# A mixer block with a long convolution: a compact constant expanded on ScalarE, q loaded by two rows, and a permutation moved up in the second chunk

## The chip, the cores and the metric

The kernel runs on one core of a Trainium2 chip. The metric is the device time of one execution in microseconds. A core has TensorE (PE, matmuls into PSUM), VectorE (DVE), ScalarE (ACT) and GpSimd (POOL) for elementwise work, and SyncE (SP), whose queue issues most of the DMA transfers here. Each engine takes its instructions in the order of the program. They wait for each other only where data or a buffer calls for it.

## The reference

All data is fp32, with S = 2048 tokens and D = 640 channels. The first half is a long causal convolution with a gate, the second a token-mixing MLP:

```python
mod = (silu(c) @ w_mod).reshape(1, 6, 1, -1)
sa, ca, ga, sb, cb, gb = (mod[:, i] for i in range(6))
h = layernorm(x) * (1 + ca) + sa                        # x = q
kv = causal_conv4(k, shift_k) * v                       # per channel
y = irfft(rfft(kv, 4096) * rfft(ssm_k, 4096))[:2048] + kv * ssm_D
x = x + ga * (h * y)
h = layernorm(x) * (1 + cb) + sb
x = x + gb * (gelu(layernorm(h).T @ w1 + b1) @ w2 + b2).T
```

## The kernel before

The channels are worked in five chunks of 128. Within a chunk each half of 64 channels is handled on its own. The convolution is a discrete transform in two steps, both as small fp32 matmuls, for the signal and for the filter.

- `step1(side, t)` is the first step: 32 matmuls into one PSUM buffer, then one ScalarE evacuation into `Z`. Side 0 is the signal (from `X`, or from `X1` for chunk 1), side 1 the filter, from `KSP`, which lies in tile `P`. Four calls make a side.
- `f2(g)`, eight calls per chunk, is the second step for both sides: 64 matmuls against the constant `W2` (tiles `w0` for g below 4 and `w1` for the others). ScalarE copies the filter's half to `kt`, VectorE makes two products into `P` (two buffers in turn), and POOL, or VectorE for the last g, adds them into `Y`.
- `i2(r)` and `i1(half)` are the two steps back. `i2` fills two PSUM buffers, which ScalarE evacuates in four instructions. `gate(c, ps, half)` multiplies the result of `i1` by the normalised q (`A1`) and adds it to x.

`psum()` hands out three PSUM buffers in turn. A matmul group that takes a buffer waits until the group three calls before it has been read.

Beside the transforms of one chunk, the next chunk's products kv are computed (`kv_ops`, on VectorE and, for one quarter, on POOL), and later chunks' rows of k and v are loaded (`kv_loads`, `load_k`, `load_v`). `load_ks(c)` loads chunk c's filter, `perm_add` (POOL) adds `ssm_D` to it, and `perm` (ScalarE, 128x2048) lays it out in `KSP`.

The order is written out by hand. Start: rows of k and v and the filter for chunk 0 (lines 450 to 461), kv for chunk 0, then the two halves of `W2` between the loads for chunk 1 (lines 481 and 483), `perm(0)`, and step one. In the loop over chunks (line 549) the calls of `f2` are mixed with other work. At the end of chunk 0, `load_q` (line 495) loads all of q into tiles `xa` and `xb`, 16 rows per partition; one DMA is one row for 64 partitions. Then `q_stats` makes the row statistics.

The modulation vectors of the first half are computed in chunk 1. `mod_load` fetches five pieces of `w_mod`, each of which needs a place: the first three go to `X1`, `KSR` and the start of `T_in`, the others wait until a place has been read. `mod_part` multiplies one piece into the PSUM tile `tap` (12 matmuls), `mod_sum` copies the sum out, and `mod_row(i)` spreads a row over 128 partitions with matmuls on one partition. `late(n)` then applies gate and normalisation to chunk 0, which could not be done before, and `ac`/`po` prepare `A1` of chunk 1 on ScalarE and VectorE.

The tile `xa` is empty until `load_q`.

Of the kernel before, what the change touches and what calls it, by code (L numbers as in the profile page):

```python
# [20 lines left out]
def _constants():  # L21
# [20 lines left out]
    sel = np.zeros((128, 128))  # L42
    sel[0, 0:64] = sel[1, 64:128] = 1
    small = np.concatenate([f1.reshape(128, 256), v2, np.eye(128)[:, 0:36], sel], 1)
    return {"small": small.astype(np.float32), "w2": w2.reshape(128, 8192).astype(np.float32),
# [4 lines left out]
def mixer_kernel(ctx: ExitStack, tc: tile.TileContext, q, k, v, shift_k, ssm_k, ssm_D, w1, b1, w2, b2, c,  # L50
# [49 lines left out]
    SM = T_v1[:, 4096:4516]  # L100
    F1, V2, ID = SM[:, 0:256], SM[:, 256:384], SM[:, 384:420]
# [354 lines left out]
    sync.dma_start(SM, dram(c_small, 0, [[548, 128], [1, 420]]))  # L456
# [22 lines left out]
    kv_loads(1, 2)  # L479
    run(kv_ops(3))  # L480
    sync.dma_start(T_w2[0], c_w2[:, 0:4096], max_dma_last_dim=4096)
# [13 lines left out]
    def load_q():  # L495

        for j in range(16):
            for b in range(2):
                sync.dma_start(XH[j // 8][64 * b:64 * b + 64, j % 8], dram(q, (16 * b + j) * D, [[32 * D, 64], [1, D]]))  # L499
# [33 lines left out]
    pl = [t[:, 0:1920] for t in (X1, KSR, T_in, KSR, T_in)]  # L533
# [15 lines left out]
    for c in range(NC):  # L549
# [3 lines left out]
        for g in range(8):  # L553
# [665 lines left out]
```

## Time and profile before

| | us |
|---|---|
| three runs | 702.47, 696.88, 701.62 |
| median of the runs | 701.62 |
| the profiled execution | 699.95 |
| its span | 698.1 |

The profiled execution is a fourth one. The profile's times count from the start of its span; the 1.85 us between span and execution lie around it. Where the stages of the first chunks lie, by TensorE's timeline:

| stage | begins, us |
|---|---|
| first matmul of step one, chunk 0 | 23.30 |
| `f2`, chunk 0 | 40.16 |
| first step back, chunk 0 | 62.77 |
| `f2`, chunk 1 | 91.68 |
| first step back, chunk 1 | 119.39 |
| filter's step one for chunk 2 | 146.91 |
| `f2`, chunk 2 | 158.42 |

Busy times over the span:

```profile
PE 624.4 (89%) x9099; PEld 597.3 (86%) x9099; DVE 494.4 (71%) x881; ACT 293.8 (42%) x469; POOL 139.5 (20%) x161
```

PEld is the loading of weights, which overlaps the matmuls. A busy share is an average over stages with different limits. What an edit is worth has to be read in its own stage: which wait ends last there, and what stands next behind it. In a timeline row the columns are the start, the duration, the engine, the line of the kernel, the operation, what it writes and reads, and a count where neighbours are merged. The brackets hold the idle time before and what ended it.

### The profile page before, as it was taken

The numbers are of one execution on the slowest core, as the hardware profiler recorded it, in microseconds if no ns is written. First come the engines' busy times: TensorE is split into PE (matmuls) and PEld (weight loads), VectorE is DVE, ScalarE is ACT, GpSimd is POOL, SyncE is SP. The second block draws the span as 40 slices with busy tenths as digits, with TensorE's granted clock in tenths as the row PEclk, the third lists the DMA queues.
The fourth block names the chain that finished last, engine by engine and source line by source line (L and its number), as shares of the span: only waits on it lengthen the run. The fifth ranks groups of instructions, "written<-read, shape, count | busy, mean of one in ns | idle before, by whom it ended". The sixth has DMA issues, their size and how long they took to land.

```text
span 698.1 us, 20773 instructions
## 1 busy us (share of the span) xinstructions
PE 624.4 (89%) x9099; PEld 597.3 (86%) x9099; DVE 494.4 (71%) x881; ACT 293.8 (42%) x469; POOL 139.5 (20%) x161
## 2 busy tenths in 40 slices
PE   0689889978799988888799999999999989999997
PEld 0688886868798878678799979999999989999997
DVE  7857976578959539888985841123399968888985
ACT  0544562665536636456666232233244233333331
POOL 5176423259125025000100000000000430000000
PEclk9999999889999999999999999999999999999999
DMA  9998788575433524161305504433353533466611
GB/s 179 242 222 222 193 254 236 119 161 124 85 73 102 164 64 122 59 152 31 60 1 92 117 5 93 89 61 62 106 143 105 158 129 100 121 171 172 174 36 38
DMA packets 166931, 84.38 MB, mean 121 GB/s; under 512 B 91030, under 2 KB 157368, under 8 KB 166840
## 3 DMA queue, kind: packets, MB, share of 16 engines
q1 hardware_dynamic: 162220, 81.72, 46.8%
q10 hardware_dynamic: 4620, 1.33, 1.1%
q8 instruction: 71, 1.16, 0.7%
q14 instruction: 20, 0.16, 0.1%
HBM read 72.55 MB, written 10.49 MB: 119 GB/s over the span
## 4 chain that ended last, share of the span: by engine, by line
PE 60%; DVE 18%; DMA 6%; ACT 5%; SPq 4%; issue 3%; POOL 3%; ACTq 0%; POOLq 0%; DVEq 0%
PE pst L438 20%; PE pst L1078 17%; PE pst L1155 7%; PE pst L220 5%; PE pst L264 4%; SPq L499 3%; DVE tap L59 3%; DVE p L59 3%; PE pst L235 3%; DVE kt L59 2%; DMA in<-in_A_k_dram 2%; DMA in<-in_A_v_dram 2%; PE pst L284 2%; PE tap L344 1%; DVE aux L59 1%
## 5 line engine op out<-in xcount | busy, mean ns | idle before, releaser
L235 PEld LDWEIGHTS pst<-z,w 128*64 128x64 f32 x2560 | 76.8, 138 | 18.3 <-issue 9.8
L235 PE MATMUL pst<-z,w 128*64 128x64 f32 x2560 | 79.2, 223 | 14.7 <-issue 5.6
L59 DVE TENSOR_TENSOR p<-pst,kt 128x512 f32<-128x512 f32 x80 | 51.2, 681 | 18.1 <-ACT kt L239 14.1
L222 ACT ACTIVATE z<-pst 128x1024 f32<-128x1024 f32 x40 | 42.9, 1073 | 46.5 <-PE pst L220 46.5
L59 POOL TENSOR_TENSOR y<-p 128x256 f32<-128x256 f32 x72 | 51.1, 739 | 49.1 <-DVE p L59 48.9
L220 PE MATMUL pst<-v,x 128*64 128x128 f32 x512 | 35.3, 301 | 27.6 <-DVE x L59 27.6
L220 PEld LDWEIGHTS pst<-v,x 128*64 128x64 f32 x512 | 32.5, 154 | 29.9 <-POOL t L465 23.3
L220 PE MATMUL pst<-v,p 128*64 128x128 f32 x640 | 40.3, 290 | 5.3 <-ACT p L163 4.4
L239 ACT ACTIVATE kt<-pst 128x512 f32<-128x512 f32 x40 | 23.9, 598 | 48.5 <-PE pst L235 33.1
L1078 PE MATMUL pst<-r_z,m_w 128*128 128x320 f32 x222 | 42.0, 312 | 2.2 <-DVE m_w L59 2.2
L220 PEld LDWEIGHTS pst<-v,p 128*64 128x64 f32 x640 | 38.5, 147 | 6.2 <-ACT p L163 4.6
L914 ACT ACTIVATE pst<-pst,sm 128x640 f32<-128x640 f32 x13 | 10.0, 767 | 75.9 <-PE pst L438 75.9
L264 PEld LDWEIGHTS pst<-v,y 32*128 32x128 f32 x1280 | 38.5, 189 | 3.9 <-issue 2.9
L264 PE MATMUL pst<-v,y 32*128 32x64 f32 x1280 | 40.4, 274 | 0.4 <-issue 0.3
L1066 ACT ACTIVATE m_w<-m_v 128x896 fp32r<-128x896 f32 x24 | 22.7, 951 | 36.9 <-PE pst L1078 16.8
L59 POOL TENSOR_TENSOR m_p<-u_i,r_z 128x320 f32<-128x320 f32 x1 | 0.9, 876 | 183.4 <-issue 183.4
L1078 PEld LDWEIGHTS pst<-r_z,m_w 128*128 128x128 f32 x222 | 35.2, 190 | 2.4 <-DVE m_w L59 2.4
L59 DVE TENSOR_TENSOR tap<-tap,kt 128x512 f32<-128x512 f32 x48 | 33.4, 697 | 1.2
L59 DVE TENSOR_TENSOR kt<-in,tap 128x512 f32<-128x512 f32 x48 | 32.9, 686 | 1.5
L273 ACT ACTIVATE z<-pst 128x512 f32<-128x512 f32 x38 | 20.9, 648 | 22.5 <-PE pst L264 22.5
L284 PEld LDWEIGHTS pst<-z,v 64*64 64x64 f32 x1280 | 22.2, 144 | 9.4 <-issue 5.8
L284 PE MATMUL pst<-z,v 64*64 64x64 f32 x1280 | 24.1, 229 | 6.7 <-issue 4.1
(301 smaller groups left out, 1483.7 us busy)
## 6 DMA issues: line engine op xcount, KB each, us to landing
x<-in_B_w_dram SPq DMA_DIRECT2D x20, 512.0 KB
aux<-in_A_ssm_k_dram SPq DMA_DIRECT2D x10, 512.0 KB
in<-in_A_k_dram SPq DMA_DIRECT2D x36, 128.0 KB
in<-in_A_v_dram SPq DMA_DIRECT2D x36, 128.0 KB
m_x<-xs SPq DMA_DIRECT2D x28, 160.0 KB
out_dram<-m_x SPq DMA_DIRECT2D x28, 160.0 KB
w<-in_const_w_dram SPq DMA_DIRECT2D x2, 2048.0 KB
m_v<-in_B_w_dram SPq DMA_DIRECT2D x9, 448.0 KB
```

The costliest lines, as they stand in the source:

```text
L59: TT = lambda eng, o, a, b, op: eng.tensor_tensor(o, a, b, op=op)
L220: pe.matmul(ps[64 * ri:64 * ri + 64, o:o + 255:2], lhs, F1[:, 128 * ri:128 * ri + 128], start=True, stop=True)
L222: evac = lambda: act.activation(Z[:, side, t], ps.rearrange("p (a k e) -> p a k e", a=4, e=2), AF.Copy)
L235: pe.matmul(ps[64 * h:64 * h + 64, o:o + 64], W2[k1 // 32][:, 2 * (k1 % 32) + ri], rhs, start=True, stop=True)
L239: act.activation(kt.rearrange("p (m i) -> p m i", i=32), pv[:, :, 1], AF.Copy)
L264: pe.matmul(pp[qd // 2][:, o:o + 64], Y[p, ri, i:i + 2].rearrange("p i k -> p (i k)"), V2[p, 64 * ri:64 * ri + 64], start=ri == 0, stop=ri ...
L284: pe.matmul(ps[64 * b:64 * b + 64, 512 * e + 64 * jj:512 * e + 64 * jj + 64], V1[p, ri, n2], T2[p, :, 32 * ri + n2], start=ri == 0, stop=r ...
L438: pe.matmul(ps[0:m, h, 0:320], w_.bitcast(F32R), r_[:, 320 * h:320 * h + 320].bitcast(F32R), start=first and i == 0, stop=last and i == 2)
L499: sync.dma_start(XH[j // 8][64 * b:64 * b + 64, j % 8], dram(q, (16 * b + j) * D, [[32 * D, 64], [1, D]]))
L1066: act.activation(W[n][0].bitcast(F32R), A[p, w_], AF.Copy)
L1078: pe.matmul(bank[n], w[:, i].bitcast(F32R), r.bitcast(F32R), start=i == 0 and k == 0, stop=i == 6 and k == 2)
L1155: pe.matmul(acc[s][:, h, 0:320], w[:, f_].bitcast(F32R), u[r + h].bitcast(F32R), start=f_ == 0 and k == 0, stop=f_ == NF - 1 and k == 2)
```

## The change

Three parts.

1. `W2` held, for each column of the transform, a copy of the coefficients for one channel of a pair and zeros for the other. The constant is now stored without the zeros, 128x4096 in place of 128x8192. Its two halves are loaded into the tile `xa`, and ScalarE lays them out in `W2`. Each instruction (`w2_part`) writes the columns of one channel, scaled per partition by 1 or 0 (`OWN`, two new columns of the small constant). Half 0 takes two instructions around step one, half 1 takes four in the first three calls of `f2`. The two loads also stand earlier in SP's queue.
2. `load_q` loads two rows per DMA. A copy of eight rows from `q` to `xs` in device memory precedes it; `xs` is overwritten later by the spilled x.
3. In chunk 1, `mod_part` starts one call of `f2` earlier, so that four of the five lie in the loop. The places of the fourth and fifth piece change, and the filter of chunk 2 is loaded in the loop. `mod_sum` writes to `T_z` in place of `P`, which lets `perm(2)` run before the first step back. The three `mod_row` calls move ahead of that step, too.

```diff
-    w2 = np.zeros((2, 32, 2, 64, 2, 2, 32))
-    for c in range(2):
-        w2[0, :, c, :, 0, c] = np.cos(ang)
-        w2[1, :, c, :, 0, c] = -np.sin(ang)
-        w2[0, :, c, :, 1, c] = np.sin(ang)
-        w2[1, :, c, :, 1, c] = np.cos(ang)
+    w2 = np.zeros((2, 32, 2, 64, 2, 32))
+    w2[0, :, :, :, 0] = np.cos(ang)[:, None]
+    w2[1, :, :, :, 0] = -np.sin(ang)[:, None]
+    w2[0, :, :, :, 1] = np.sin(ang)[:, None]
+    w2[1, :, :, :, 1] = np.cos(ang)[:, None]
...
+    own = np.arange(128)[:, None] % 2 == np.arange(2)
+    small = np.concatenate([f1.reshape(128, 256), v2, np.eye(128)[:, 0:36], own], 1)
...
+    def w2_load(i):
+        sync.dma_start(T_x[0][:, 2048 * i:2048 * i + 2048], c_w2[:, 2048 * i:2048 * i + 2048])
+
+    def w2_part(i, c_, o=0, n=64):
+        act.activation(T_w2[i].rearrange("p (m c k) -> p c m k", c=2, k=32)[:, c_, o:o + n],
+                       T_x[0][:, 2048 * i + 32 * o:2048 * i + 32 * (o + n)].rearrange("p (m k) -> p m k", k=32),
+                       AF.Identity, scale=OWN[:, c_:c_ + 1])
...
     run(kv_ops(2, pool))
+    w2_load(0)
     run(kv_ops(0))
     kv_loads(1, 0)
     run(kv_ops(1))
     kv_loads(1, 1)
     kv_loads(1, 2)
+    w2_load(1)
     run(kv_ops(3))
-    sync.dma_start(T_w2[0], c_w2[:, 0:4096], max_dma_last_dim=4096)
     kv_loads(1, 3)
-    sync.dma_start(T_w2[1], c_w2[:, 4096:8192], max_dma_last_dim=4096)
     perm_add(0)
     perm(0)
+    w2_part(0, 0)
     all_taps()
     for t in range(4):
         step1(0, t)
+        if t == 1:
+            w2_part(0, 1)
...
-        for j in range(16):
+        sync.dma_start(dram(xs, 0, [[8 * D, 8], [1, 8 * D]]), dram(q, 0, [[8 * D, 8], [1, 8 * D]]))
+        for j in range(0, 16, 2):
             for b in range(2):
-                sync.dma_start(XH[j // 8][64 * b:64 * b + 64, j % 8], dram(q, (16 * b + j) * D, [[32 * D, 64], [1, D]]))
+                sync.dma_start(XH[j // 8][64 * b:64 * b + 64, j % 8:j % 8 + 2],
+                               dram(q, (16 * b + j) * D, [[32 * D, 64], [D, 2], [1, D]]))
...
-    pl = [t[:, 0:1920] for t in (X1, KSR, T_in, KSR, T_in)]
+    pl = [t[:, 0:1920] for t in (X1, KSR, T_in, X1, T_in)]
...
+            if c == 0 and g < 3:
+                for i in ((0, 1), (2,), (3,))[g]:
+                    w2_part(1, i % 2, 32 * (i // 2), 32)
...
-                if g > 4:
-                    mod_part(tap, g - 5, three(pl[g - 5]))
-                    if g > 5:
-                        mod_load(0, g - 3, pl[g - 3])
+                if g > 3:
+                    mod_part(tap, g - 4, three(pl[g - 4]))
+                if g == 4:
+                    mod_load(0, 3, pl[3])
+                if g == 6:
+                    mod_load(0, 4, pl[4])
+                    load_ks(2)
...
             step1(0, 0)
-            mod_part(tap, 3, three(pl[3]))
-            load_ks(2)
+            mod_part(tap, 4, three(pl[4]))
+            mod_sum(tap, T_z[:, 5120:5760])
             step1(0, 1)
-            mod_part(tap, 4, three(pl[4]))
...
             q_newton(3)
-            mod_sum(tap, P[:, 0:640])
+            mod_row(0, T_z[:, 5120:5760])
+            mod_row(1, T_z[:, 5120:5760])
+            perm_add(2)
+            perm(2)
+            load_ks(3)
+            mod_row(2, T_z[:, 5120:5760])
             i2(0)
-            mod_row(0, P[:, 0:640])
-            mod_row(1, P[:, 0:640])
-            mod_row(2, P[:, 0:640])
             run(late(2)[0] + ac[0:4])
...
             spill(0)
-            perm_add(2)
-            perm(2)
-            load_ks(3)
             taps()
```

More of the change, by code (lines that the diff above doesn't have):

```diff
@@ L41, in _constants @@
     v1 = np.tile(np.stack([np.cos(ang), np.sin(ang)], 1).reshape(64, 4096) / 2048, (2, 1))
[L42 to L45, printed above, removed]
+    own = np.arange(128)[:, None] % 2 == np.arange(2)
+    small = np.concatenate([f1.reshape(128, 256), v2, np.eye(128)[:, 0:36], own], 1)
+    return {"small": small.astype(np.float32), "w2": w2.reshape(128, 4096).astype(np.float32),
             "v1": v1.astype(np.float32)}
@@ L99, in mixer_kernel @@
     V1 = T_v1[:, 0:4096].rearrange("p (r n m) -> p r n m", r=2, n=32)
-    SM = T_v1[:, 4096:4516]
-    F1, V2, ID = SM[:, 0:256], SM[:, 256:384], SM[:, 384:420]
+    SM = T_v1[:, 4096:4518]
+    F1, V2, ID, OWN = SM[:, 0:256], SM[:, 256:384], SM[:, 384:420], SM[:, 420:422]
     TR, DR = T_rows[:, 0:256], T_rows[:, 512:576]
@@ L455, in mixer_kernel @@
         load_v(0, g, both)
-    sync.dma_start(SM, dram(c_small, 0, [[548, 128], [1, 420]]))
+    sync.dma_start(SM, dram(c_small, 0, [[422, 128], [1, 422]]))
     load_ks(0, act)
```

## The prediction

> **What bounds the kernel now.** I read the page's chain of waits first, then the timelines of the engines and of SP's queue over the first 200 us, because every edit lies in the program's first 160 us. What comes after is the same code, and it starts when these stages end.
>
> ```profile
> PE 60%; DVE 18%; DMA 6%; ACT 5%; SPq 4%; issue 3%; POOL 3%; ACTq 0%; POOLq 0%; DVEq 0%
> ```
>
> TensorE holds most of the path. So an edit counts where TensorE stands still in the stages it touches, or where it takes work off TensorE. There are three such places. The first is the second transform (`f2`) of chunk 0. POOL computes a quarter of chunk 1's product there, and only then makes the additions that free `f2`'s buffers:
>
> ```profile
> 38.29 2.50 POOL L59 TENSOR_TENSOR t<-in,t 128x512 f32<-128x512 f32 x2 [15.15 <-DMA in<-in_A_v_dram]
> ...
> 48.86 6.98 POOL L59 TENSOR_TENSOR y<-p 128x256 f32<-128x256 f32 x10
> ```
>
> ```profile
> 49.63 1.39 DVE L59 TENSOR_TENSOR p<-pst,kt 128x512 f32<-128x512 f32 x2 [2.95 <-POOL y L59]
> ```
>
> POOL stood 15.15 us for a transfer, so its additions begin at 48.86, and VectorE's third product of `f2` waits 2.95 us for them. The second place is the end of chunk 1, in TensorE's own timeline:
>
> ```profile
> 102.48 2.08 PE L235 MATMUL pst<-z,w 128*64 128x64 f32 x64 [1.25 <-DVE p L59]
> ...
> 118.18 1.28 PE L344 MATMUL tap<-in,sm 128*32 128x320 f32 x12 [0.24 <-DMA in<-in_w_mod_dram]
> 119.39 3.80 PE L264 MATMUL pst<-v,y 32*128 32x64 f32 x128
> 123.01 4.83 PE L355 MATMUL pst<-p,sm 1*128 1x320 f32 x12
> 127.77 3.68 PE L220 MATMUL pst<-v,x 128*64 128x128 f32 x32
> 131.38 4.21 PE L264 MATMUL pst<-v,y 32*128 32x64 f32 x128
> 135.52 1.97 PE L220 MATMUL pst<-v,x 128*64 128x128 f32 x32
> ...
> 146.91 3.68 PE L220 MATMUL pst<-v,p 128*64 128x128 f32 x32 [4.44 <-ACT p L163]
> 150.93 6.34 PE L220 MATMUL pst<-v,p 128*64 128x128 f32 x96 [0.34 <-DVE aux L59]
> ```
>
> The columns are start, duration, instructions, and in brackets the idle time before and what ended it. The wait of 4.44 us for the permutation (ACT `p`) looks like the prize. But the 96 matmuls after it start only at 150.93, when the gate (DVE `aux`) has freed a PSUM buffer. The permutation lies beside the gate's own chain. The third place is two gaps with no releaser:
>
> ```profile
> 48.86 1.33 PE L235 MATMUL pst<-z,w 128*64 128x64 f32 x38 [2.06 <-issue]
> ...
> 81.00 1.31 PE L284 MATMUL pst<-z,v 64*64 64x64 f32 x41 [2.19 <-issue]
> ```
>
> Both fall while long-row transfers run (the second half of `w`, and `q`). I take them, as a guess, for TensorE waiting for its own instructions.
>
> **Step two's matrix.** Removed are two loads of 2.1 MB. Added are two of 1.05 MB and six ScalarE instructions. In SP's queue:
>
> ```profile
> 18.93 1.85 SPq L137 DMA_DIRECT2D in<-in_A_v_dram  x2
> ...
> 27.31 0.64 SPq L481 DMA_DIRECT2D w<-in_const_w_dram  x1
> 28.05 1.54 SPq L131 DMA_DIRECT2D in<-in_A_k_dram  x2
> ```
>
> The k and v rows that POOL waits for are issued from 28.05, right behind the first `w` load. After the change the same 2.1 MB is ahead of them, but half of it is issued at 18.93 or earlier, and the engines have room there:
>
> ```profile
> 20.00:28.00 8.00, 4.70 (x58) 4.73 (x60) 5.82 (x10) 4.44 (x3) 1.43 (x2) 1.00 0.76 166
> 30.00:34.00 4.00, 4.00 (x78) 4.00 (x76) 3.79 (x7) 2.37 (x3) 0.00 (x0) 1.00 1.02 410
> ```
>
> The last two numbers of a row are the DMA share and GB/s. From 20 to 28 us the 16 engines are 0.76 busy, so (1 - 0.76) x 8 = 1.9 us is free. Behind that, `w` moves at 410 GB/s, so one load takes 1.05 MB / 410 GB/s = 2.6 us. POOL's rows come earlier by what the free time absorbs: 1.9 us, at most 2.6, and nothing if its wait is paced by something else on SP's queue. I take 1.9 because that room is a measured share. It is less than the 2.95 us that VectorE waits, so all of it passes on to the end of `f2`, and TensorE, busy from there to 90 us, carries it on. What is late next is ScalarE's copy of `f2`'s result, which the new instructions share.
>
> ```profile
> 22.84 2.06 ACT L163 ACTIVATE p<-aux 128x2048 f32<-128x2048 f32 x1
> ...
> 28.58 1.09 ACT L222 ACTIVATE z<-pst 128x1024 f32<-128x1024 f32 x1 [0.66 <-PE pst L220]
> ...
> 44.16 0.60 ACT L239 ACTIVATE kt<-pst 128x512 f32<-128x512 f32 x1 [1.27 <-PE pst L235]
> ```
>
> Two of the instructions take 2048 elements, like the permutation at 22.84 (2.06 us each), and four take 1024, half of that (1.03 each): 8.2 us in all. The first is queued behind the permutation, so ready at 24.9, and all eight evacuations of step one stand behind it. Its load is issued by 18.93 + 0.64 = 19.6 and needs 2.6 us of engines that are no longer full then, so it lands between 22 and 24. Step one gives ScalarE one evacuation per 1.09 + 0.66 = 1.75 us, and three PSUM buffers are in turn. Part, two evacuations, part, third evacuation take 2 x 2.06 + 3 x 1.09 = 7.4 us. TensorE wants the third buffer again at 28.58 + 3 x 1.75 = 33.8, so the cover is gone only if the load lands after 26.4, and then the cost is one for one. The other four follow the evacuations of `f2`, between which ScalarE idles 1.27 us. They make the second evacuation under 1 us late, inside VectorE's 2.95 us wait. I cost ScalarE's work at nothing.
>
> **q by two rows.** 32 issues become 17, behind one copy from `q` into `xs` on eight engines.
>
> ```profile
> 73.22 12.45 SPq L499 DMA_DIRECT2D xa<-in_A_q_dram  x16
> 85.71 11.54 SPq L499 DMA_DIRECT2D xb<-in_A_q_dram  x16
> ```
>
> SP issues q for 24.0 us, 5.24 MB, so 218 GB/s. Behind it stand the loads of `w_mod`. The change starts q sooner and at best halves it. On TensorE's path the late loads cost only the 0.24 us at 118.18, so the edit is worth 0.24 us, and nothing if q is no faster. The spill of chunk 0, which overwrites what the copy put into `xs`, is issued after all of q has been used.
>
> **Chunk 1's order.** Before, three `mod_part`s lie in `f2` and two behind it. After, four and one. The extra one (1.28 us) fits the gap of 1.25 us at 102.48, so the loop is no longer. Step one's second group then ends at 117.94 as before, with the last `mod_part` already done. From there, before: 0.24 + 1.28, inverse 3.80, rows 4.83, step one 3.68, inverse 4.21, end 135.6. After: rows, inverse, evacuation of both its PSUM buffers with step one beside it, inverse. The clock decides what these cost:
>
> ```profile
> 118.00:124.00 6.00, 5.82 (x144) 4.64 (x144) 0.00 (x0) 2.50 (x4) 0.50 (x2) 1.00 1.06 171
> 124.00:127.00 3.00, 2.91 (x9) 1.78 (x8) 0.00 (x0) 3.00 (x7) 0.00 (x0) 0.74 0.65 148
> 127.00:130.00 3.00, 3.00 (x24) 2.23 (x24) 2.02 (x3) 2.67 (x7) 0.00 (x0) 0.50 0.82 185
> 130.00:133.00 3.00, 3.00 (x58) 2.67 (x54) 2.90 (x5) 1.08 (x1) 1.10 (x1) 0.62 0.20 46
> ```
>
> The third number from the end is the granted clock. At 0.50 for the rest of 124 to 127, all of 127 to 130 and part of 130 to 133, it was half for 1.56 + 3 + 2.28 = 6.8 us, a loss of 3.4 us. It fell inside the twelve row matmuls, which use one partition, and the 32 matmuls of step one took 3.68 instead of 1.97 us. At full clock the rows cost 4.83 less half of the 2.4 us after 125.4, so 3.6 us.
>
> ```profile
> 135.63 2.22 ACT L273 ACTIVATE z<-pst 128x512 f32<-128x512 f32 x4 [3.06 <-PE pst L264]
> ```
>
> With the evacuation at 2.22 the new order ends at 117.94 + 3.6 + 3.80 + 2.22 + 3.80 = 131.4, plus a clock loss between 0 and 3.4. I take 2.0, since the same rows still run in one block. Gain 135.6 - 133.4 = 2.2 us (0.8 to 4.2), and the gate's chain follows it.
>
> [...]
>
> The permutation moves ahead of the inverse's evacuations, and ScalarE now waits there for `ssm_k`, chunk 2:
>
> ```profile
> 116.09 3.73 SPq L151 DMA_DIRECT2D aux<-in_A_ssm_k_dram  x2
> ```
>
> Its 1.05 MB moves at 171 GB/s until 124, 8 us after issue. Now it is issued behind the fifth `w_mod` load, which waits for the third `mod_part`: 102.48 + 2 x (2.08 + 1.28) = 109.2, so it lands by 118. ScalarE reaches the permutation after two of the three row groups, 117.94 + 2.4 = 120.3, and the inverse whose evacuation stands behind it ends at 117.94 + 3.6 + 3.80 = 125.3 or later: nothing is lost. POOL's small addition moves with it, ahead of additions that need the rows' result. The next filter load moves up in SP's queue and waits for the permutation; behind it stand v loads that wait for VectorE's work on those rows.
>
> Taking the permutation off the end gives nothing, as shown above. It costs something: TensorE does the first group at 146.91 - 4.44 = 142.5, relative to before, then idles 150.93 - 142.5 - 1.97 = 6.5 us up to the gate, and the next 32 matmuls run at half clock, 3.68 - 1.97 = 1.7 us more. Before, that was paid inside the wait (3.68 at 146.91). Of this,
>
> ```profile
> 167.09 1.39 DVE L59 TENSOR_TENSOR p<-pst,kt 128x512 f32<-128x512 f32 x2 [0.77 <-POOL y L59]
> ```
>
> 0.8 us is hidden, since VectorE waits for POOL in chunk 2 anyway. Cost 0.9 us (0 to 1.7).
>
> **Sum**, against the profiled execution of 699.95 us (span 698.1): -1.9 - 2.2 + 0.9 = -3.2, so 696.7 us. That execution is 1.7 us under the median of the runs, 701.62. About 1%, 7.0 us, is what a measurement of this kernel can tell from no change: faster means under 694.6, slower over 708.6.
>
> **Rivals.** *More is gained.* The row matmuls leave the clock alone (2.0 more), POOL gains 2.6 (0.7 more), the half-clock cost is hidden (0.9 more), and the gap at 81.00 vanishes because q is in by then (2.19 more): 696.7 - 5.8 = 690.9. For: q starts sooner by the whole stage. Against: the rows still stand in one block. Chance 0.23.
>
> *Nothing is gained.* POOL's wait ends with a v transfer issued after 28.05, and if SP's queue paces it, not the bytes, the 1.9 is gone; with a clock loss of 3.4 chunk 1 gives 0.8 and loses 0.9. Time 700.1. Chance 0.17. A variant is that the eight-engine copy does nothing for q, which leaves every number as it is.
>
> *Slower: TensorE's unnamed gaps multiply.* If long rows starve it, q (now beside the two inverses of chunk 0, which run 128 matmuls in under 5 us) does it more often. A gap costs 2.1 us and, with the clock halved behind it, 1.7 more. One extra gap cancels the gain (700.5); four give 696.7 + 15.2 = 711.9. For: both gaps lie beside such loads. Against: these two are the only ones of 2 us in the timeline of the first 200 us. Chance 0.13, mostly above 708.6.
>
> **Numbers.** The forecast, 696.7, has 0.47; its own range by the terms' bounds is 693 to 700. The range for 8 in 10 takes in the first two rivals and one extra gap: 689 to 702. Faster by over 1%: the first rival and a tenth of the forecast, 0.28. Slower by over 1%: 0.09. Within 1%: 0.63.
>
> **What would show it.** Right: POOL's 15.15 us wait is about 13 and VectorE's 2.95 is near 1; no TensorE wait on `z` evacuations before 40 us; five `mod_part`s done before step one's second group; no idle of ScalarE before the third permutation; half clock at the gate's first 32 matmuls. Wrong: ScalarE waiting for `xa` at 25 us, new TensorE gaps of 2 us named issue between 57 and 80, or a full clock behind the rows.

## The result and the profile after

| | us |
|---|---|
| before, median of its runs beside the changed kernel | 701.67 |
| changed kernel, median of 4 runs (708.1 to 710.13) | 709.41 |
| ratio, 95% interval | 1.0123, 1.0075 to 1.017 |
| span of the profiled execution, before and after | 698.1, 707.7 |

The change costs about 8.6 us by the ratio, 7.7 by the medians. Executions over 1.5% longer than the fastest of the same kernel are left out of all ratios here. The forecast was 696.7 and the range ended at 702. What came is the event of the rival on the slower side: more and longer gaps without a releaser on TensorE. The page's chain of waits of the changed kernel, shares of the span by engine:

```profile
PE 71%; DVE 15%; ACT 5%; issue 5%; DMA 3%; POOL 1%; DVEq 0%; ACTq 0%; POOLq 0%
```

"issue", time for which the trace knows no releaser, rose from 3% to 5%. TensorE's timeline of the changed kernel shows where, between the second inverse of chunk 0 and the filter's step one:

```profile
68.48 4.04 PE L262 MATMUL pst<-v,y 32*128 32x64 f32 x120
75.17 0.71 PE L262 MATMUL pst<-v,y 32*128 32x64 f32 x8 [2.64 <-issue]
75.80 3.68 PE L218 MATMUL pst<-v,aux 128*64 128x128 f32 x32
79.42 1.74 PE L282 MATMUL pst<-z,v 64*64 64x64 f32 x88
84.16 3.69 PE L282 MATMUL pst<-z,v 64*64 64x64 f32 x128 [3.01 <-issue]
92.83 1.34 PE L282 MATMUL pst<-z,v 64*64 64x64 f32 x40 [4.97 <-issue]
94.10 8.62 PE L218 MATMUL pst<-v,p 128*64 128x128 f32 x128
```

Before there was one gap here, 2.19 us at 81.00. Now there are three, 10.62 us in all, and behind them the clock is down for a while: step one's 32 matmuls at 75.80 take 3.68 us, with a granted clock of 0.51 from 76 to 80; at 1.00, as at 128.01, they take 1.97. The matmuls come in portions of 128 (8 + 32 + 88 from 75.17, 128 from 84.16, then 40 + 88), one portion every 9.0 and 8.7 us. The windows over the same time give TensorE's busy time first and, as the last three numbers, the granted clock, the DMA share and GB/s. Before:

```profile
76.00:80.00 4.00, 2.73 (x171) 2.46 (x164) 3.83 (x6) 1.11 (x2) 2.66 (x3) 1.00 0.74 208
80.00:84.00 4.00, 3.00 (x57) 2.88 (x58) 3.86 (x9) 1.10 (x1) 0.00 (x0) 0.64 0.73 208
```

After:

```profile
72.00:76.00 4.00, 1.36 (x26) 1.10 (x24) 3.79 (x7) 0.10 (x1) 2.92 (x3) 0.64 1.04 228
76.00:80.00 4.00, 4.00 (x54) 3.67 (x55) 3.86 (x8) 2.52 (x5) 0.00 (x0) 0.51 1.02 223
80.00:84.00 4.00, 1.15 (x79) 1.01 (x72) 3.83 (x13) 0.59 (x1) 0.00 (x0) 0.92 1.04 231
88.00:92.00 4.00, 0.00 (x0) 0.00 (x0) 0.31 (x2) 0.00 (x0) 0.00 (x0) 0.50 1.03 237
```

q moves at nearly the same rate in both (208 GB/s before, 223 to 237 after), but the 16 engines were 0.73 busy and are now busy all the time, at 1.02 to 1.04. SP issues q's loads of two rows from 64.81 to 81.06, in 16.3 us in place of 24.0, and the share stays over 1 up to 96 us: the queue is full. Instructions are among what the 16 engines move. The view of the DMA queues for 64 to 100 us has them as a kind of their own (packets, MB, share of the 16 engines), before:

```profile
q8 instruction: 8, 0.13, 1.7%
```

and after:

```profile
q8 instruction: 5, 0.08, 1.0%
```

That TensorE waited for these packets can be read from their times, which the trace has for each one. Queue 8 moves 71 packets of 16 KB over the whole span, and TensorE executes 9099 matmuls and as many weight loads. 9099 / 71 is 128, so by this estimate one packet holds some 128 matmuls with their loads: the portion. In the changed kernel:

| packet on queue 8, from and to, us | TensorE goes on at, us | after a gap of, us |
|---|---|---|
| 72.46 to 73.77 | 75.17 | 2.64 |
| 81.26 to 82.52 | 84.16 | 3.01 |
| 90.05 to 91.28 | 92.83 | 4.97 |

Each time TensorE goes on 1.4 to 1.6 us after a packet has landed. The gap before, at 81.00, ends in the same way behind a packet that landed at 79.61. From 22 to 290 us, the 17 traces of this case have 117 gaps of 0.8 us or more named "issue"; all of them end 1.2 to 1.7 us after a packet of queue 8 has landed. The packets themselves take no longer than before, 1.2 to 1.3 us against 1.0 to 1.5. They start later: 8.8 us apart beside the full queue, 3.8 to 5.0 us apart before, from 61 to 88 us.

By TensorE's timelines the 9.6 us between the two spans lie as follows (each stage by its start times, after less before):

| stage | us |
|---|---|
| start of `f2`, chunk 0 | +1.3 |
| `f2`, chunk 0 | -1.2 |
| from there to `f2`, chunk 1 (steps back of chunk 0, step one) | +12.1 |
| `f2`, chunk 1, to `f2`, chunk 2 | -1.1 |
| the rest | -1.5 |

Of the 12.1 us, 8.4 are gaps (10.62 less 2.19). 3.6 are matmuls at half clock behind them: step one's 32 cost 1.7 more, the 128 at 84.16 took 3.69, with a granted clock of 0.50 from 84 to 88, where 128 at 1.00 take 2.10 (e7, at 79.51), so 1.6, and the rest adds 0.3. Of the first row, 0.3 us is a later first matmul (23.60 after 23.30), and 1.0 is step one, whose 128 matmuls took 9.71 us in place of 8.74. In the other runs with the same new instructions it took from 8.5 to 10.1, in those without them from 8.5 to 9.0. So the change may have a part in it, and the runs don't settle how much.

The second inverse stage, in the changed kernel's timeline:

```profile
128.01 1.97 PE L218 MATMUL pst<-v,x 128*64 128x128 f32 x32
129.91 2.55 PE L353 MATMUL pst<-z,sm 1*128 1x320 f32 x12
132.09 5.91 PE L262 MATMUL pst<-v,y 32*128 32x64 f32 x128
137.93 3.64 PE L218 MATMUL pst<-v,x 128*64 128x128 f32 x32
141.50 3.80 PE L262 MATMUL pst<-v,y 32*128 32x64 f32 x128
...
160.66 7.70 PE L218 MATMUL pst<-v,p 128*64 128x128 f32 x96 [5.15 <-DVE aux L57]
```

From the end of step one's second group to the end of the second inverse it takes 145.30 - 129.98 = 15.3 us. The clock falls as before, but behind the rows: it is 0.76, 0.50 and 0.60 in the three windows of 3 us from 133 to 142, the inverse takes 5.91 in place of 3.80 and step one 3.64 in place of 1.97.

And the part of the matrix, in the timelines of POOL, VectorE and TensorE of the changed kernel:

```profile
37.23 2.52 POOL L57 TENSOR_TENSOR t<-in,t 128x512 f32<-128x512 f32 x2 [14.26 <-DMA in<-in_A_v_dram]
```

```profile
48.62 1.39 DVE L57 TENSOR_TENSOR p<-pst,kt 128x512 f32<-128x512 f32 x2
```

```profile
53.02 3.95 PE L233 MATMUL pst<-z,w 128*64 128x64 f32 x127 [1.23 <-issue]
58.10 1.32 PE L233 MATMUL pst<-z,w 128*64 128x64 f32 x38 [1.13 <-issue]
```

POOL starts 1.1 us earlier, and VectorE's third product no longer waits for it. But TensorE now has two gaps inside `f2`, 1.23 and 1.13 us, where before had one of 2.06 at 48.86 and two of 0.32.

### The profile page after: what moved, and what is told of

It reads as the page before. It is cut to its first block, busy times and chain, and to the rows that moved or that the text cites. A ratio compares the mean times of both kernels' runs of the same rounds, so it can differ in the third digit from the quotient of the medians.

```text
span 707.7 us, 20734 instructions
## 1 busy us (share of the span) xinstructions
PE 629.5 (89%) x9099; PEld 604.2 (85%) x9099; DVE 492.9 (70%) x881; ACT 301.5 (43%) x475; POOL 139.3 (20%) x161
## 4 chain that ended last, share of the span: by engine, by line
PE 71%; DVE 15%; ACT 5%; issue 5%; DMA 3%; POOL 1%; DVEq 0%; ACTq 0%; POOLq 0%
PE pst L436 19%; PE pst L1093 17%; PE pst L218 10%; PE pst L1170 7%; PE pst L233 6%; PE pst L262 6%; PE pst L282 3%; DVE p L57 2%; DVE tap L57 2%; PE tap L342 1%; DVE aux L57 1%; PE pst L966 1%; DVE kt L57 1%; DVE sm L559 1%; DMA in<-in_w_mod_dram 1%
## 5 line engine op out<-in xcount | busy, mean ns | idle before, releaser
L218 PE MATMUL pst<-v,x 128*64 128x128 f32 x512 | 37.6, 313 | 28.4 <-DVE x L57 27.9
L218 PEld LDWEIGHTS pst<-v,x 128*64 128x64 f32 x512 | 34.7, 161 | 30.2 <-POOL t L463 23.6
L262 PE MATMUL pst<-v,y 32*128 32x64 f32 x1280 | 41.9, 279 | 2.8 <-issue 2.6
```

The lines of the kernel that those rows point to most:

```text
L218: pe.matmul(ps[64 * ri:64 * ri + 64, o:o + 255:2], lhs, F1[:, 128 * ri:128 * ri + 128], start=True, stop=True)
L262: pe.matmul(pp[qd // 2][:, o:o + 64], Y[p, ri, i:i + 2].rearrange("p i k -> p (i k)"), V2[p, 64 * ri:64 * ri + 64], start=ri == 0, stop=ri ...
```

## The experiments

Each was measured beside the kernel before on its own chip, so the ratio is what counts. "One row" means q as in the kernel before.

| run | what it is | ratio to before | interval |
|---|---|---|---|
| e1 | after, q by one row, no copy | 1.0014 | 0.9989 to 1.0038 |
| e2 | after, no copy | 1.0087 | 1.005 to 1.0124 |
| e3 | after, copy's rows apart | 1.0115 | 1.0037 to 1.0193 |
| e4 | before + q by two rows | 1.0093 | 1.0062 to 1.0125 |
| e5 | before + matrix | 0.9981 | 0.9951 to 1.0011 |
| e6 | before + order of chunk 1 | 1.0053 | 1.0024 to 1.0083 |
| e7 | after, q paced | 1.0094 | 1.0059 to 1.0129 |
| e8 | after, q to 128 partitions | 0.9989 | 0.9927 to 1.0052 |
| e9 | after, q in packets of 2560 B | 1.0152 | 1.0127 to 1.0176 |
| e10 | before + rows on 96 partitions | 0.9981 | 0.9958 to 1.0004 |
| e11 | e1 + rows on 96 partitions | 0.9936 | 0.9913 to 0.9959 |
| e12 | e5 + rows on 96 partitions | 0.9944 | 0.9916 to 0.9972 |
| e13 | after + rows on 96 partitions | 1.0105 | 1.0068 to 1.0141 |
| e14 | after, half of q later | 1.0127 | 1.0072 to 1.0183 |
| e15 | e11, constant of the inverse later | 0.9907 | 0.9877 to 0.9938 |

### Which part costs: e1 to e4

```diff
# e1, against after
-        sync.dma_start(dram(xs, 0, [[8 * D, 8], [1, 8 * D]]), dram(q, 0, [[8 * D, 8], [1, 8 * D]]))
-        for j in range(0, 16, 2):
+        for j in range(16):
...
-                sync.dma_start(XH[j // 8][64 * b:64 * b + 64, j % 8:j % 8 + 2],
-                               dram(q, (16 * b + j) * D, [[32 * D, 64], [D, 2], [1, D]]))
+                sync.dma_start(XH[j // 8][64 * b:64 * b + 64, j % 8], dram(q, (16 * b + j) * D, [[32 * D, 64], [1, D]]))
# e2 takes out the first line alone; e4 is before with the lines of after
# e3, against after
-        sync.dma_start(dram(xs, 0, [[8 * D, 8], [1, 8 * D]]), dram(q, 0, [[8 * D, 8], [1, 8 * D]]))
+        sync.dma_start(dram(xs, 0, [[16 * D, 8], [1, 8 * D]]), dram(q, 0, [[16 * D, 8], [1, 8 * D]]))
```

> The changed kernel with q loaded by one row again and without the copy (the other two parts kept). Theory A, a full transfer queue behind two-row loads of q keeps TensorE's own instructions waiting: the three gaps named issue between 70 and 95 us (10.6 us together) shrink to at most one of about 2 us, f2 of chunk 1 begins near 92 us, and the time is 697 to 701 us, level with or just under the kernel before. Theory B, the earlier start of q (the W2 part frees SP's queue) or chunk 1's new order makes the loss: the gaps stay near 10 us, or the loss stands elsewhere, and the time stays at 707 to 710.

> The changed kernel without the copy from q to xs; q stays at two rows per load. Theory A (the two-row loads fill the queue): nothing changes beyond the 0.16 MB that go, 708 to 710 us, three gaps of about 10 us together, q still moves at about 225 GB/s. Rival C (the copy is what delays TensorE's instructions, as it writes device memory): the gaps shrink to 2 to 3 us and the time falls to 698 to 702.

> The changed kernel with the copy's eight rows 16 rows apart, so that they cannot be joined into one run and cut into sixteen; as it stands, the lowered copy has 16 pieces of 10 KB and lies on 16 engines, not 8. Theory D (the copy was meant to put eight engines one transfer behind the other eight, so that both partition halves are written at once, and does not because it runs on sixteen): q now moves at 330 to 420 GB/s in place of 225, is in by about 80 us, the gaps fall to 2 to 5 us together and the time to 697 to 703. Rival (the rate of q is not set by the halves): 225 GB/s and 708 to 710 us as before.

> The kernel before with only the q part (copy and two-row loads). Theory A: q starts at 73 us as before and its queue is full until about 97, beside i1, step one and f2 of chunk 1; TensorE's gaps named issue between 75 and 100 us rise from 2.2 to 6 to 12 us and the time to 704 to 712. Theory B (the loss comes from the other parts): within 2 us of the kernel before, 699 to 704.

With q by one row the loss is gone (e1), and q by two rows alone makes it (e4). In e1 one gap is left here:

```profile
82.82 0.81 PE L282 MATMUL pst<-z,v 64*64 64x64 f32 x40 [1.57 <-issue]
...
91.89 6.51 PE L233 MATMUL pst<-z,w 128*64 128x64 f32 x215 [1.12 <-ACT z L220]
```

The start of `f2` of chunk 1 says the same: 91.89 us in e1 and 103.03 in e4, whose profiled execution was the longest of its ten. But e1, which keeps the other two parts, is not faster than before either, though the forecast gave these two parts 3.2 us, a ratio of 0.995. The copy is not the cause (e2). Nor does it come in eight pieces in the changed kernel: from 64 to 68 us the trace has 1180 packets, 1161 of them under 8 KB, and of the 19 others 3 are instructions, which leaves 16 for the 160 KB of the copy; 14 of them are on their way at once, at 66.0 us. With the rows apart (e3), 8 such packets are left, but q's rate stays at 226 to 232 GB/s, the share at 1.02, and the gaps are 2.09 and 6.30 us. So the copy in eight packets does nothing for q; on how many engines they lie, the trace does not say.

### Full queue, length of the packets, or rate: e7, e9, e8

```diff
# e7: a load of 256 bytes ahead of each, which reads what the load two before it has brought
+            if n >= 2:
+                jo, bo = (n - 2) // 2 * 2, (n - 2) % 2
+                sync.dma_start(dram(xs, 256 * D + 64 * n, [[64, 1], [1, 64]]), XH[jo // 8][64 * bo:64 * bo + 1, jo % 8 + 1, 0:64])
# e9
-                               dram(q, (16 * b + j) * D, [[32 * D, 64], [D, 2], [1, D]]))
+                               dram(q, (16 * b + j) * D, [[32 * D, 64], [D, 2], [1, D]]), max_dma_last_dim=2560)
# e8: eight loads in place of sixteen
+            sync.dma_start(XH[j // 8][:, j % 8:j % 8 + 2], dram(q, j * D, [[16 * D, 128], [D, 2], [1, D]]))
```

> The changed kernel with q's two-row loads paced: ahead of each stands a load of 256 bytes that reads what the load two before it has brought, so that only two are on their way, in place of all that SP's queue takes. Theory depth (rows of 5 KB waiting in the 16 engines' queues hold up TensorE's instructions): the gaps named issue between 57 and 100 us fall from 10.6 us to under 4, f2 of chunk 1 starts near 93 instead of 103.8, and the time is 700 to 703. Theory size (one 5 KB row ahead of the instructions is enough, whatever waits behind it): the gaps stay at 8 us or more and the time at 707 to 711. Rival rate: if the DMA share stays over 0.95 with two on their way, the queue is full all the same, and the run does not tell the two apart.

> The changed kernel with q's two-row loads cut into packets of 2560 bytes, one row each; the order, the sixteen loads and the copy are as in the changed kernel. Theory size (5 KB packets hold up the instructions): the gaps between 57 and 100 us fall to before's level, 2 to 4 us, and the time to 700 to 703. Theory full queue (the instructions come late whenever the sixteen engines are busy all the time, whatever the packets): the DMA share from 72 to 88 us stays at 1.0, the gaps at 8 us or more, the time at 707 to 711.

> The changed kernel with q by eight loads of two rows for 128 partitions in place of sixteen for 64 (the partitions get other rows of q than the reference's, so the output differs from it; bytes and row length are the same). If the 225 GB/s of q is set by the half of the partitions that a load writes, q moves at 350 to 410 GB/s here, is in within 15 us instead of 27, and the gaps beside it fall in number: under 6 us in all between 57 and 100, f2 of chunk 1 near 97 or earlier, the time 701 to 705. If the rate is set by the row length or by the source, q stays at 225 GB/s and the time at 708 to 711.

Shorter packets change nothing (e9): its windows and timeline have the full queue and the gaps, 8.14 us in these two.

```profile
84.00:88.00 4.00, 0.00 (x0) 0.00 (x0) 3.83 (x13) 0.00 (x0) 0.00 (x0) 0.77 1.06 242
```

```profile
79.76 3.43 PE L282 MATMUL pst<-z,v 64*64 64x64 f32 x128 [2.91 <-issue]
88.42 1.34 PE L282 MATMUL pst<-z,v 64*64 64x64 f32 x40 [5.23 <-issue]
```

With the loads paced (e7) the packets are as long as in the changed kernel, but the queue runs empty between them (the share is 0.56 from 72 to 80 us), and the gaps go back to before's level, 2.44 us. So do the instruction packets from 64 to 100 us, 8 again:

```profile
76.00:80.00 4.00, 3.50 (x148) 3.12 (x148) 3.79 (x7) 2.62 (x5) 0.79 (x1) 1.00 0.56 134
```

```profile
q8 instruction: 8, 0.13, 1.6%
```

```profile
79.51 2.10 PE L282 MATMUL pst<-z,v 64*64 64x64 f32 x128 [0.26 <-issue]
83.78 0.81 PE L282 MATMUL pst<-z,v 64*64 64x64 f32 x40 [2.18 <-issue]
...
107.64 2.36 PE L342 MATMUL tap<-aux,sm 128*32 128x320 f32 x12 [5.23 <-DMA aux<-in_w_mod_dram]
```

`f2` of chunk 1 starts at 92.86, as expected of "depth". But the time is 1.0094, not 700 to 703: q so slowed holds up `w_mod` behind it, and TensorE waits 5.23 us for that by name. The half clock behind the rows then lasts some 20 us (0.61 from 130 to 133, 0.50 in every window from there to 151), and from step one's second group to the second inverse's end it takes 19.4 us, in e1 15.3. Half of the expectation held. Since pacing lowers both the number on the way and the share, the runs name the full queue, and don't part these two.

Eight loads for 128 partitions (e8) move q at

```profile
72.00:76.00 4.00, 3.89 (x115) 3.68 (x112) 3.83 (x6) 2.75 (x3) 3.83 (x3) 1.00 1.00 403
```

where the changed kernel has 223 to 237 GB/s with rows of the same length: the 225 GB/s of q go with the 64 partitions that each load writes there. The gaps do not vanish, since the queue is full here too, with a share of 1.00 to 1.04 from 72 to 88 us: 1.87 and 4.38 us, with the portions 6.5 us apart (80.80, 87.27). Its ten executions spread from 696.5 to 732.0 us around a median of 707.6, and its ratio rests on three of them, so its time decides nothing.

### The other two parts: e5 and e6

```diff
# e6, against before: the third part of the change alone
-    pl = [t[:, 0:1920] for t in (X1, KSR, T_in, KSR, T_in)]
+    pl = [t[:, 0:1920] for t in (X1, KSR, T_in, X1, T_in)]
...
+                if g > 3:
+                    mod_part(tap, g - 4, three(pl[g - 4]))
...
+            mod_row(0, T_z[:, 5120:5760])
+            mod_row(1, T_z[:, 5120:5760])
+            perm_add(2)
+            perm(2)
+            load_ks(3)
+            mod_row(2, T_z[:, 5120:5760])
             i2(0)
# e5, against before: the first part alone (w2_load, w2_part, OWN)
```

> The kernel before with part 1 alone (step two's matrix laid out by ScalarE; q by one row, chunk 1 in the old order). By the prediction's first term: f2 of chunk 0 ends 1.9 us earlier and the time is 700.3 - 1.9, so about 699. By the rival that f2 is held by TensorE's instruction stream and not by POOL: VectorE's wait for POOL shrinks from 2.95 us to under 1, but issue gaps of about 1 us in f2 of chunk 0 take it back, because the loads for the inverse now lie beside f2; the time is within 1 us of before. If the six instructions of ScalarE or the load behind them cost something on the path, it is slower by that amount, and TensorE or ScalarE waits for the tile of the constant near 25 us.

> The kernel before with part 3 alone (chunk 1's order). By the prediction: -2.2 and +0.9, so 1.3 us under before. By the reading of the changed kernel's trace: the half clock lasts through the first inverse (5.9 instead of 3.8 us) and step one (3.6 instead of 2.0), so from the rows to the second inverse's end nothing or less than 1 us is gained, and the first 96 matmuls after the gate take 7.5 us instead of 6.3; the time is within 1 us of before, or up to 1 us slower. q keeps its one-row loads, so the gaps between 57 and 100 us stay at 2 to 5 us in all.

The matrix alone (e5) is worth 1.3 us by its ratio, between a gain of 3.4 and a loss of 0.8: not told apart from nothing, nor from the 1.9 us of the forecast. In its trace POOL's additions begin at 47.86, 1.0 us earlier than before, and VectorE waits 1.13 us for them. Yet the first inverse begins later than in before's profile, at 64.39 in place of 62.77, behind a gap inside `f2` and a wait for VectorE's `aux`:

```profile
53.22 6.55 PE L233 MATMUL pst<-z,w 128*64 128x64 f32 x165 [2.06 <-issue]
60.74 3.71 PE L218 MATMUL pst<-v,aux 128*64 128x128 f32 x64 [0.96 <-DVE aux L57]
64.39 3.80 PE L262 MATMUL pst<-v,y 32*128 32x64 f32 x128
```

The order alone (e6) costs 3.7 us (1.7 to 5.8), more than either theory expected. Its profiled execution was the longest of its twelve, 3.8 us over their median, so the sizes below hold for that one. Its timeline:

```profile
103.22 1.28 PE L344 MATMUL tap<-aux,sm 128*32 128x320 f32 x12 [3.09 <-DMA aux<-in_w_mod_dram]
...
121.26 2.55 PE L355 MATMUL pst<-z,sm 1*128 1x320 f32 x12
123.44 6.68 PE L264 MATMUL pst<-v,y 32*128 32x64 f32 x128
130.05 3.68 PE L220 MATMUL pst<-v,x 128*64 128x128 f32 x32
133.66 7.11 PE L264 MATMUL pst<-v,y 32*128 32x64 f32 x128
140.70 3.68 PE L220 MATMUL pst<-v,x 128*64 128x128 f32 x32
```

Two things show. With q by one row `w_mod` comes later, and the first `mod_part`, now one call of `f2` earlier, waits 3.09 us for it. And the half clock lasts from 125 to 145 us, through both inverses, though TensorE's matmuls leave no gap: its windows there are 3.00 of 3 us busy.

```profile
133.00:136.00 3.00, 3.00 (x52) 2.67 (x52) 2.08 (x3) 3.00 (x7) 0.07 (x1) 0.50 1.23 196
139.00:142.00 3.00, 3.00 (x48) 2.88 (x46) 0.00 (x0) 1.14 (x3) 0.00 (x0) 0.50 0.76 172
```

### What halves the clock: e10 to e13

```diff
+    part = small(3)          # 1/32 in rows 32 j to 32 j + 31 of column j, else 0
...
+            if i < 3:
+                pe.matmul(ps[:, h, 0:320], part[0:96, j:j + 1].to_broadcast([96, 128]),
+                          t[0:96, 320 * h:320 * h + 320], start=True, stop=True)
+                continue
             pe.matmul(ps[:, h, 0:320], ones[32 * j:32 * j + 1, 0:1].to_broadcast([1, 128]),
                       t[32 * j:32 * j + 1, 320 * h:320 * h + 320], start=True, stop=True)
```

> The kernel before with one edit: the twelve matmuls that spread the modulation rows work on 96 partitions in place of one. The 32 copies of each sum that already lie there are weighted by 1/32, and the other rows by 0, so the result is the same. Theory: the chip lowers the clock because matmuls on one partition keep too little of TensorE busy, though it never idles; then the granted clock stays at 1.00 from 121 to 133 us, the rows take 2.5 us in place of 4.83 and step one 2.0 in place of 3.68, and the second inverse ends some 3.4 us earlier, less what the gate then waits longer; the time is 1 to 3 us under before. Rival: the clock falls for another reason (the inverse on 32 partitions ahead of the rows, or a fixed time after a wait): then 0.50 is seen from 125 to 132 us as before, and the time is the same.

> The changed kernel with q by one row again (as in the run of that kind) and the rows on 96 partitions. If the rows are what halves the clock, the first inverse behind them takes 3.8 us (6.26 with the rows on one partition) and step one 2.0 (3.28), and the part of the order is worth what the prediction said without a clock loss: the second inverse ends 3.4 us earlier than in that run, the time is 698 to 700. The clock still falls at the gate, behind a real wait of 5 us. If the clock falls all the same, the time is 702 to 703 as in that run.

> The kernel before with part 1 (step two's matrix) and the rows on 96 partitions, nothing else: a candidate for a version faster than both. The gain of the rows, 1 to 3 us, and of part 1, 0 to 1.9 us, add up if each stands: 697 to 700 us.

> The changed kernel with the modulation rows on 96 partitions, nothing else. The clock stays at 1.00 from the rows to the second inverse (half for 6.5 us in the changed kernel, so 3.3 us lost). If the terms add, the time is 709.4 - 3.3 = 706, with the gaps beside q's loads as large as before the edit (8 to 11 us between 57 and 100 us): the loss against before is then q's alone, and more than the whole of it. If it falls to 702 or less, the half clock and not the gaps made most of the loss.

In e10 the same twelve matmuls at the same place, on 96 partitions, leave the clock at 1.00 (TensorE's timeline, then the windows):

```profile
124.10 3.70 PE L357 MATMUL pst<-p,sm 96*128 96x320 f32 x12
127.73 1.97 PE L221 MATMUL pst<-v,x 128*64 128x128 f32 x32
```

```profile
124.00:127.00 3.00, 3.00 (x18) 1.92 (x15) 0.00 (x0) 2.79 (x6) 0.00 (x0) 1.00 0.56 119
127.00:130.00 3.00, 3.00 (x47) 2.31 (x50) 2.05 (x3) 3.00 (x8) 0.00 (x0) 1.00 0.87 196
```

and in e11, in the new order:

```profile
119.53 3.50 PE L355 MATMUL pst<-z,sm 96*128 96x320 f32 x12
122.96 3.80 PE L263 MATMUL pst<-v,y 32*128 32x64 f32 x128
126.69 1.97 PE L219 MATMUL pst<-v,x 128*64 128x128 f32 x32
```

So here it is the matmuls on one partition behind which the clock falls. TensorE's weight loads pause in the rows, for ScalarE to free PSUM, but by no more than 0.60 us before, and from 124 to 127 us they are busy for 1.78 us before and 1.92 in e10. In e10 the span from the first inverse's start to the second's end shrinks from 16.20 to 13.06 us; at the gate some of it is given back, and the time is 1.3 us under before (from 2.9 under to 0.3 over). e11 and e12 are faster than before beyond their intervals. In place the edit is worth 2.1 us, not the 3.4 expected: from step one's second group to the second inverse's end it is 13.2 us in e11 and 15.3 in e1, since the rows on 96 partitions take 122.96 - 119.53 = 3.4 us where those on one took 2.2. By the ratios the step from e1 to e11 is 0.8%, known to some 0.3%. In e13's trace the half clock is gone as well (1.00 in every window from 118 to 157 us), the inverse behind the rows takes 3.80 us. But from the changed kernel to e13 it is 0.2%, known to 0.6%, so no gain is shown there, and the 706 us expected did not come. e13 also answers what q's part costs without the half clock of the rows: its gaps between 57 and 100 us are 9.6 us, and it stays 1.0% over before.

### Where the full queue lies, and a faster version: e14 and e15

```diff
# e14, against after: the second half of q and w_mod behind the last step back
+            sync.dma_start(dram(xs, 256 * D, [[64, 1], [1, 64]]), T_in[0:1, 4224:4288])
+        for j in range(8 * half, 8 * half + 8, 2):
...
-            for kk in range(3):
-                mod_load(0, kk, pl[kk])
             for half in range(2):
                 ps = i1(half)
...
+            load_q(1)
+            for kk in range(3):
+                mod_load(0, kk, pl[kk])
# e15, against e11
-    sync.dma_start(T_v1[:, 0:4096], c_v1, max_dma_last_dim=4096)
...
                 load_v(2, g)
+                if g == 1:
+                    sync.dma_start(T_v1[:, 0:4096], c_v1, max_dma_last_dim=4096)
```

> The changed kernel with q's second half and the three loads of w_mod behind chunk 0's last step back (a load of 256 bytes that reads its result holds them up); loads, lengths and the sixteen issues are the same. Theory pace (beside a full queue instructions come at 128 matmuls in 8.7 us, 15 per us; the last step back needs 61 per us, step one 16, the second transform 31): the two gaps in or ahead of the last step back go, down to the 2 to 3 us of before; step one's 128 matmuls for the filter, now beside the full queue, take under 9 us; gaps of together 2 to 5 us come up in f2 of chunk 1, beside the end of q and w_mod. f2 of chunk 1 starts at 91 to 96 and the time is 702 to 706. Theory amount (each transfer costs its part wherever it lies): the gaps between 57 and 115 us are 9 us or more in all, and the time is 708 to 711.

> The kernel with parts 1 and 3, q by one row and the rows on 96 partitions (697 us), with the load of the inverse's constant (2.1 MB) moved behind the first two loads of chunk 2's rows, from 45 to about 54 us. Theory: that load beside f2 of chunk 0 made the gap near 53 us (1.8 us), and it ate what part 1 gained. Then f2 of chunk 0 has no gap over 1 us near 53, ends 1 to 2 us earlier, and the time is 695 to 696. If the gap stays or moves into f2's end, the time is the same, 697. If the constant comes too late for the first inverse at 64 us, that waits for it by name and the time is longer.

e14 agrees with "pace" in where things move and not in the time: 1.0127 is what "amount" gave, though the gaps from 57 to 115 us are 8.1 us, under its 9. One gap stays in the last step back, the other moves into `f2`, beside the rest of q and `w_mod`:

```profile
80.19 4.27 PE L282 MATMUL pst<-z,v 64*64 64x64 f32 x168 [3.18 <-issue]
...
103.29 4.80 PE L233 MATMUL pst<-z,w 128*64 128x64 f32 x105 [4.05 <-issue]
```

`f2` of chunk 1 starts at 92.73, as expected; then the second gap, a late piece of `w_mod` (1.10 us) and the half clock of the rows (0.65, 0.50, 0.50 and 0.64 in the windows from 127 to 139) take it back. Step one, meant to lie beside the full queue, did not: from 80 to 88 us the share was 0.2 or less. That it can live with the slow instructions is argued from its need (32 matmuls in 1.97 us, 16 per us, against 128 in 8.7 us, 15 per us) and shown only in short: in the kernel before, from 28 to 36 us, the share was 0.97 and 1.13 and TensorE, in step one, was busy throughout.

e15 is the fastest of all, 0.9% under before. In its profiled execution, the longest of twelve, no gap named "issue" is left in `f2` of chunk 0. TensorE waits there for VectorE instead, 1.05 us for `p` and 1.95 for `aux`:

```profile
50.73 5.82 PE L234 MATMUL pst<-z,w 128*64 128x64 f32 x192 [1.05 <-DVE p L57]
58.50 3.71 PE L219 MATMUL pst<-v,aux 128*64 128x128 f32 x64 [1.95 <-DVE aux L57]
```

The first inverse starts at 62.14 us, in e11 at 64.26. From the start of `f2` that is 22.1 us, which e12 has with the early load, too. The next gap is 2.73 us at 80.42. The intervals of e11 and e15 overlap, so the edit is shown to remove its gap, and not to save time.

## Why the prediction was wrong

**q by two rows: the step that failed.** "On TensorE's path the late loads cost only the 0.24 us at 118.18, so the edit is worth 0.24 us, and nothing if q is no faster." The step weighed when q arrives and left out what else uses the DMA engines meanwhile. q was no faster (223 to 237 GB/s with loads for 64 partitions, 403 in e8 with loads for 128), but the queue that had been 0.73 busy became full, at 1.02 to 1.04. TensorE's instruction packets then started 8.8 us apart, and TensorE stood still for them. e4 has this alone, at 1.0093; e1 without it, at 1.0014. The sign of being wrong that the prediction named, a new gap of 2 us between 57 and 80 us, came at 75.17.

**The other 3.2 us.** They did not come either: e1 has both other parts and not q's, and its interval, 0.9989 to 1.0038, leaves out 0.995. So q explains the loss against before and not the whole distance to the forecast.

**The rival had the event and half of its price.** It put 2.1 us of gap and 1.7 of half clock on each further gap. Two further gaps came, with 8.4 us of gap and 3.6 of half clock: the clock as priced, the gaps twice as long. Its reason, long rows, was not the cause: beside packets of 2560 bytes TensorE stands still as well (8.14 us in e9), and beside rows of 5 KB, two loads at a time, for no longer than in before (2.44 us in e7). It got 0.13 because there were only two gaps in the first 200 us. That count said little: both lay in stages that take many matmuls per us (31 and 61), and what kept them few was SP, which needed 24 us to issue 32 loads. The windows of before show that as a share of 0.73 beside q. The change takes away just that.

**The matrix.** The first half of the mechanism held: POOL came 1.1 us earlier, not 1.9, and VectorE's wait for it went in the changed kernel and fell to 1.13 us in e5. ScalarE's six instructions cost TensorE no wait that the trace shows, as forecast. The first found its load in place at 24.85 us, and behind the third and fourth the second copy of `f2` came 0.7 us late, inside the room that the prediction had for it. What failed is "all of it passes on to the end of `f2`". What is late next is TensorE's instructions, beside the constant of the inverse, which SP now issues 9.0 us earlier (44.76 in place of 53.79). From the start of `f2` to the first inverse the changed kernel's profile has 21.4 us in place of 22.6. But e5 has 24.1, and the profiles of all runs with the matrix lie between 21.4 and 24.8, those without it between 22.1 and 25.8. A gain is not shown.

**Chunk 1's order.** Forecast from step one's second group to the second inverse's end: 133.4 - 117.94 = 15.5 us; measured 15.3. Two of its terms were off and cancelled. The rows cost 2.2 us, not 3.6: in before's 4.83 us their weight loads had waited 1.2 us, 0.8 of it for ScalarE's `z`, which the prediction read as work. And the clock cost 3.8 by the lengths (2.1 in the inverse, 1.7 in step one) or 3.4 by the granted clock of the windows, not 2.0: the upper bound of 3.4 or beyond. e1 has the same 15.3 us and loses it on both sides: from the start of `f2` to step one's second group it takes 28.1 us in place of 26.3, with a gap of 1.53 us and 0.88 us of waiting for `w_mod`, and the way to the next `f2` is 1.2 us longer. e6 shows the order as a loss where `w_mod` comes late and the half clock lasts 20 us.

**The clock.** In before TensorE was busy for 2.91 of the 3 us from 124 to 127 and for 3.00 of the next 3, and the granted clock was 0.74 and 0.50. e10 adds what counts: with the rows on 96 partitions it was busy for 3.00 of both, and the clock was 1.00. So at nearly equal busy time the clock halved behind matmuls on one partition and not behind those on 96.

**The permutation.** Forecast +0.9, bounds 0 to 1.7; from the second inverse's end to `f2` of chunk 2 it is 24.2 us in place of 22.8, so +1.4, with the gate's 5.15 us wait and 96 matmuls in 7.70 instead of 6.34 us.

**Open.** Why an instruction packet that moves in 1.3 us starts only 8.8 us after the one before it when the queue is full. Why the half clock behind the rows lasts 6.8 us in the changed kernel, some 10 in e14 and 20 in e6 and e7. Whether a full queue with little on its way would starve TensorE as well.

## What to carry to other kernels

Before making transfers longer or fewer, look at the DMA share of the stage and at what the slow issue was good for: here TensorE lost 2.2 us beside a queue that was 0.73 busy and 10.6 beside a full one. Where a change fills it, count gaps named "issue" as a term of the sum, above all beside stages that take many matmuls per us (here, beside q, the gaps lay where TensorE takes 30 and 61). Where a few rows are spread over the partitions by matmuls on one partition, look at the clock behind them: in e11, on 96 partitions, with zeros as weights, they took 1.2 us longer than in e1, the clock stayed at 1.00, and the stage was 2.1 us shorter.

## What the runs showed of the hardware that was not expected

Beside DMA engines kept full by q (share 1.02 to 1.04), TensorE got its instructions in portions of 128 matmuls every 8.7 to 9.0 us, every 6.5 us where q went to 128 partitions (e8), and every gap of 0.8 us or more, from 22 to 290 us in all the traces, ended 1.2 to 1.7 us after an instruction packet had landed. Packets of 2560 bytes in place of 5120 didn't help (gaps of 8.14 us in e9), loads issued two at a time did (2.44 us in e7). The granted clock fell to 0.50 though TensorE's weight loads paused by no more than 0.60 us in the rows of before: it fell behind twelve matmuls on one partition, and behind the same twelve on 96 it stayed at 1.00 (e10). Through the inverse on 32 partitions and step one behind them it stayed there for 20 us in e6 and e7; by itself, in chunk 0 of the kernel before, that inverse ran at 1.00, in 4.13 us.
